# Attention over a cached K and V: keys loaded two units at a time, in even and odd partitions

## The chip, the cores and the metric

The kernel runs on one core of a Trainium2 chip. The metric is the device time of one execution in microseconds (us). Three runs of the kernel before gave 185.0, 185.05 and 185.06 us; the median is 185.05 us. Inside the core, TensorE (PE in the profile) multiplies matrices, VectorE (DVE), ScalarE (ACT) and GpSimd (POOL) work on vectors, and SyncE (SP) issues the transfers, which 16 DMA engines carry out. Each engine works through its own instructions in their order.

## The reference

It is one step of grouped-query attention against a cache: 8 batches with 4 query tokens each, 32 query heads, 8 K/V heads, 2048 cached keys, head size 128, all in bf16.

```python
q = (x @ wq).reshape(B, Sq, Hq, Dh).transpose(0, 2, 1, 3)   # B 8, Sq 4, Hq 32, Dh 128
k = repeat(k_cache, 4, axis=1)                              # k_cache, v_cache: 8, 8, 2048, 128
v = repeat(v_cache, 4, axis=1)
p = softmax(einsum("bhqd,bhkd->bhqk", q, k) * 128 ** -0.5)
o = einsum("bhqk,bhkd->bhqd", p, v)
out = o.transpose(0, 2, 1, 3).reshape(B, Sq, 4096) @ wo     # wo: 4096, 512
```

K and V are 33.5 MB each and wq and wo 4.2 MB each, and every byte is read once.

## The kernel before

The work is cut into NU = 16 units. A unit is one batch with G = 4 K/V heads (half of the eight). Its K fills 128 partitions: partition `g * 32 + s` holds 64 successive keys of head g, 16 KiB in a row of memory. V lies the same way. K has a ring of three buffers in one tile (`k_sb`), V a pool of three (`vpool`).

For a unit, `turn_keys` (L141) has DVE transpose 32x32 blocks of 4-byte words, in NT = 2 instructions of 2048 words a partition; the results go to a pool of three `kt` tiles. `scores` (L211) makes 8 matmuls of 512 columns for each, into a PSUM tile `s_ps` of two banks, of which there are two. `maxima` (L232) takes the row maximum on DVE, `exponentials` (L251) has ACT write the exponentials `s_sb` and their sums `l_sb`. `sums` (L283) adds the two halves' sums on POOL. `probs_to_keys` (L262) transposes `s_sb` on DVE and copies 8 pieces into one of two `probs` tiles, four on ACT and four on POOL. `inverses` (L290) is a reciprocal on DVE that waits for `sums`. `values` (L297) is 32 matmuls of 256 columns against V, in four quarters. `divide` (L317) scales the result on ACT, and `finish` (L327) turns it by a matmul and copies it to `oT` on DVE. At the end the outputs are turned twice more (`to_tokens`, `to_wo_rows`) and multiplied by wo (`project`).

The order on every engine is the order in which the program is written. The main loop (L394) takes one unit a turn. Turn n does `sums(n-1)`, the two `turn_keys(n)`, `scores(n)`, `probs_to_keys(n-1)`, `inverses(n-1)`, `maxima(n)`, `exponentials(n)`, and all of `values(n-2)`. So the scores of a unit stand beside the softmax of the unit before it, and its values come two turns later. Loads are all issued by SP in one queue: K of unit 0, wq, x, K of units 1 and 2, V of unit 0, and then by `load_ready` (L122) K and V in turn, as buffers come free. The last wo rows arrive in pieces of 5, 2 and 1 rows of a partition (L393).

Of the kernel before, what the change touches and what calls it, by code (L numbers as in the profile page):

```python
# [8 lines left out]
BF16 = mybir.dt.bfloat16  # L9
# [5 lines left out]
def kernel(  # L15
# [20 lines left out]
    C = Sk // S  # L36
    HQ = rep * Sq
    NQ = G * HQ
    NT, CT = 2, C // 2
    HP = 8  # L40
    WR = 8
    NP = Hq // HP
    DH = D // 2
    NU = (Hkv // G) * B
    KB, VB, PB, LAG = 3, 3, 2, 2
    XR = 8
    scale = float(Dh) ** -0.5
    AX = mybir.AxisListType.X
# [5 lines left out]
    align.tile([128, 192], BF16, name="pad")  # L54
    wpool = ctx.enter_context(tc.tile_pool(name="wpool", bufs=1))
    kpool = ctx.enter_context(tc.tile_pool(name="kpool", bufs=1))
    vpool = ctx.enter_context(tc.tile_pool(name="vpool", bufs=VB))
    ktpool = ctx.enter_context(tc.tile_pool(name="ktpool", bufs=3))
    const = ctx.enter_context(tc.tile_pool(name="const", bufs=1))
    small = ctx.enter_context(tc.tile_pool(name="small", bufs=2))  # L60
# [5 lines left out]
    order = ctx.enter_context(tc.manual_schedule())  # L66

    wq_sb = wpool.tile([128, R, HqDh], BF16, tag="w", name="wq_sb")
    x_sb = ktpool.tile([128, CT, 2, S, 2], BF16, tag="kt", name="x_sb")
    xT_sb = const.tile([128, R, T], BF16, name="xT_sb")  # L70
    q_bd = const.tile([128, Hkv // G, 2, 2, B, G, HQ], BF16, name="q_bd")
    probs = [const.tile([128, 2, C // 4, 2, G, HQ], BF16, name=f"probs{i}") for i in range(PB)]
# [6 lines left out]
    out_sb = const.tile([T, D], BF16, name="out_sb")  # L79

    units = [(hq, b) for hq in range(Hkv // G) for b in range(B)]
    ks = [None] * NU
    vs = [None] * NU

    k_sb = kpool.tile([128, KB, C, Dh], BF16, name="k_sb")

    def load_k(u, n=1):
        hq, b = units[u]
        nc.sync.dma_start(
            k_sb[:, u % KB : u % KB + n, :, :].rearrange("p b c d -> p b (c d)"),  # L90
            k_cache[b : b + n, G * hq : G * hq + G].rearrange(
                "b g (s c) d -> (g s) b (c d)", c=C
            ),
        )
        for i in range(n):
            ks[u + i] = k_sb[:, (u + i) % KB, :, :]

    def load_v(u):
        hq, b = units[u]
        vs[u] = vpool.tile([128, C, Dh], BF16, tag="v_sb", name="v_sb")  # L100
        of = v_cache[b, G * hq : G * hq + G].rearrange("g (s c) d -> (g s) c d", c=C)
        nc.sync.dma_start(vs[u][:, :, :], of)

    def load_wo(p, r0, n):
        rows = wo[p * HP * 128 : (p + 1) * HP * 128, :].rearrange("(q r) j -> q r j", r=WR)
# [2 lines left out]

    load_k(0)
    nc.sync.dma_start(wq_sb[:, :, :], wq.rearrange("(p r) n -> p r n", r=R))  # L110
    x_all = x_sb[:T, :, :, :, :].rearrange("q c h s e -> q (c h s e)")
    nc.vector.memset(x_all, 0.0)  # L112
    nc.sync.dma_start(x_all[::XR, :], x.flatten_outer_dims().rearrange("(a i) d -> a (i d)", i=XR))
    load_k(1, 2)
    loads = [("v", 0)]
    for u in range(3, NU + 2):
        if u < NU:
            loads.append(("k", u))
        loads.append(("v", u - 2))
    loads.reverse()  # L120

    def load_ready(nk, nv):  # L122
        while loads:
            kind, u = loads[-1]
            if u >= (nk + KB if kind == "k" else nv + VB):
                return
            (load_k if kind == "k" else load_v)(u)
            loads.pop()

    load_ready(0, 0)  # L130

    make_identity(nc, ident[:])
    make_identity(nc, ident4[:])
# [4 lines left out]

    kts = {}

    def turn_keys(u, t):  # L141
        kts[(u, t)] = ktpool.tile([128, CT, 2, S, 2], BF16, tag="kt", name="kt")
        nc.vector.transpose(  # L143
            kts[(u, t)][:, :, :, :, :].rearrange("k c h s e -> k (c h s e)").bitcast(FP32),
            ks[u][:, t * CT : (t + 1) * CT, :].rearrange("s c d -> s (c d)").bitcast(FP32),
        )

    for t in range(NT):
        turn_keys(0, t)

    xtp = psum_m.tile([128, R, T], FP32, tag="m", name="xtp")
    for i in range(XR):
        row = x_all[:, i * D : (i + 1) * D].rearrange("q (p r) -> q r p", r=R)
        for r in range(R):
# [5 lines left out]
                stop=True,  # L160
            )
    nc.vector.tensor_copy(out=xT_sb[:, :, :], in_=xtp[:, :, :])  # L162

    def q_products(hq):
        psq = psum_m.tile([128, rep * Dh], FP32, tag="m", name="psq")
        for r in range(R):
            for g in range(G):
                c0 = (hq * G + g) * rep * Dh
                nc.tensor.matmul(  # L169
                    psq[g * T : (g + 1) * T, :],  # L170
                    lhsT=xT_sb[:, r, :],
                    rhs=wq_sb[:, r, c0 : c0 + rep * Dh],
                    start=(r == 0),
                    stop=(r == R - 1),
                )
        return psq
# [31 lines left out]
    s_pss = {}  # L208
    less = {}

    def scores(u, t):  # L211
        hq, b = units[u]
        if t == 0:
            s_pss[u] = psum_s.tile([128, NT, CT // 2, S], FP32, tag="s", name="s_ps")
        for i in range(4):
            k, e = i // 2, i % 2
            for h in range(2):
                nc.tensor.matmul(  # L218
                    s_pss[u][h * NQ : (h + 1) * NQ, t, :, :],
                    lhsT=q_bd[:, hq, k, e, b, :, :].rearrange("k g q -> k (g q)"),  # L220
                    rhs=kts[(u, t)][:, h * CT // 2 : (h + 1) * CT // 2, k, :, e],
                    start=(i == 0),
                    stop=(i == 3),
                )
# [7 lines left out]
    def maxima(u):  # L232
        top = small.tile([128, 1], FP32, tag="top", name="top")
        swapped = small.tile([128, 1], FP32, tag="swapped", name="swapped")
        less[u] = small.tile([128, 1], FP32, tag="less", name="less")
        nc.vector.reduce_max(  # L236
            out=top[:, :],
            in_=s_pss[u][:, :, :, :].rearrange("q t c s -> q (t c s)"),
            axis=AX,
        )  # L240
        swap_halves(nc.vector, swapped, top)
        nc.vector.tensor_scalar(  # L242
            out=less[u][:, :],
            in0=swapped[:, :],
            scalar1=top[:, 0:1],
            scalar2=-1.0,
            op0=mybir.AluOpType.max,
            op1=MULT,
        )

    def exponentials(u):  # L251
        s_sbs[u] = small.tile([128, C // 4, S, 2], BF16, tag="s_sb", name="s_sb")
        l_sbs[u] = totals.tile([128, 1], FP32, tag="l_sb", name="l_sb")
        nc.scalar.activation(  # L254
            out=s_sbs[u][:, :, :, :].rearrange("q a s j -> q a j s"),
            in_=s_pss[u][:, :, :, :].rearrange("q t (a j) s -> q (t a) j s", j=2),
            func=EXP,
            bias=less[u][:, 0:1],
            accum_out=l_sbs[u][:, :],
        )  # L260
# [22 lines left out]
    def sums(u):  # L283
        swapped = small.tile([128, 1], FP32, tag="l_swapped", name="l_swapped")
        total = small.tile([128, 1], FP32, tag="l_total", name="l_total")
        swap_halves(nc.gpsimd, swapped, l_sbs[u])
        nc.gpsimd.tensor_tensor(out=total[:, :], in0=l_sbs[u][:, :], in1=swapped[:, :], op=ADD)
        return total
# [8 lines left out]
    def values(u, quarter):  # L297
        if quarter == 0:
            o_pss[u] = psum_o.tile([128, 2, Dh], FP32, tag="o", name="o_ps")
        t, h = quarter // 2, quarter % 2  # L300
        for a in range(CT // 4):
            c = quarter * C // 4 + 2 * a
            nc.tensor.matmul(  # L303
                o_pss[u][:, :, :].rearrange("n j d -> n (j d)"),
                lhsT=probs[u % PB][:, h, t * CT // 4 + a, :, :, :].rearrange(
                    "s j g q -> s (j g q)"
                ),
                rhs=vs[u][:, c : c + 2, :].rearrange("s c d -> s (c d)"),
                start=(c == 0),
                stop=(c == C - 2),  # L310
            )
# [78 lines left out]
                    stop=(p == NP - 1 and r == WR - 1),  # L390
                )

    pieces = [(0, 0, 8), (1, 0, 8), (2, 0, 8), (3, 0, 5), (3, 5, 2), (3, 7, 1)]  # L393
    for n in range(NU + LAG):  # L394
        w = n - LAG
        if 0 < n <= NU:
            total = sums(n - 1)
        if 0 < n < NU:
            turn_keys(n, 0)
            turn_keys(n, 1)  # L400
        if n < NU:
            scores(n, 0)
        if w >= 1 and n < NU:
            finish(w - 1)
        if n < NU:
            scores(n, 1)
        if n == 2:
            q_ps = q_products(1)
        if n == 3:
            spread_q(1, q_nat, [by_gpsimd] * G)  # L410
        if 0 < n <= NU:
            probs_to_keys(n - 1)
            inverses(n - 1, total)
        if n < NU:
            maxima(n)
            exponentials(n)
        if n == 2:
            q_nat = scale_q(q_ps)
        if w == B + 1:
            to_tokens(0)  # L420
        if w == B + 2:
            to_wo_rows(0)
        if w >= 0:
            for quarter in range(4):
                values(w, quarter)
            if n >= NU:
                finish(w - 1)
            (divide_all if w == NU - 1 else divide)(w)
        load_ready(min(n + 1, NU), max(w + 1, 0))
        if n == NU - 1:  # L430
            assert not loads, loads
            for piece in pieces:
                load_wo(*piece)

    out_ps = [psum_s.tile([128, DH], FP32, tag="s", name="out_ps") for _ in range(2)]
    half = WR // 2
# [42 lines left out]
```

## Time and profile before

| what | value |
|---|---|
| median of three runs | 185.05 us |
| the profiled execution: its time | 185.0 us |
| its span in the profile | 183.1 us |
| granted TensorE clock, mean | 0.925 |
| bytes read | 75.53 MB, 413 GB/s over the span |
| DMA engines' busy share (data queue) | 97.1% |
| PE, DVE, ACT, POOL busy | 123.2, 121.2, 77.9, 59.3 us |

The page gives the busy time of each engine, the span in 40 slices, the DMA queues, the chain of work that ended last, the costliest groups of instructions (mean time of one, and what ended the idle time before them) and the transfers. The time line gives single instructions with their starts. "Issue to landing" of a transfer includes the time in which it stands behind others.

### The profile page before, as it was taken

The page shows a single profiled execution, that of the slowest core. Times are in us where ns is not written, and L with a number is a line of the kernel's source. Part 1 is how long each engine was busy: PE and PEld are TensorE (multiplying, and loading weights), DVE is VectorE, ACT ScalarE, POOL GpSimd, SP SyncE. Part 2 cuts the span into 40 slices and gives each one's busy share as a digit, 9 for nine tenths or more (in the row PEclk, how much of TensorE's full clock was granted, in tenths as well). Part 3 has the DMA queues.
Part 4 walks back from the last instruction along what each step waited for, and adds up shares of the span by engine and source line. Part 5 has one row for each costly group of instructions (what it writes and reads, how often), then busy time and mean ns, then how long its engine had stood idle before and what let it go on. Part 6 is the DMA issues. An engine that isn't in the chain of part 4 may idle for free.

```text
span 183.1 us, 2559 instructions
## 1 busy us (share of the span) xinstructions
PE 123.2 (67%) x962; PEld 80.4 (44%) x962; DVE 121.2 (66%) x157; ACT 77.9 (43%) x136; POOL 59.3 (32%) x127
## 2 busy tenths in 40 slices
PE   0000652709997978869396878397776978399993
PEld 0000320303664736647154455256463656268872
DVE  6380027797989899894967768576948594946120
ACT  2000112264547748548154544529281719075030
POOL 8900020343237525415151514224240506056000
PEclk9999999995899999999969699969997599969999
DMA  6989999999999999999999999999999999999991
GB/s 182 497 386 419 426 433 429 433 433 426 429 429 437 429 431 420 438 419 437 426 433 429 433 426 437 422 437 433 426 433 429 429 433 426 433 426 422 426 392 49
DMA packets 5666, 75.70 MB, mean 413 GB/s; under 512 B 628, under 2 KB 788, under 8 KB 1044
## 3 DMA queue, kind: packets, MB, share of 16 engines
q1 hardware_dynamic: 5656, 75.57, 97.1%
q8 instruction: 7, 0.11, 0.2%
q14 instruction: 3, 0.02, 0.0%
HBM read 75.53 MB, written 0.03 MB: 413 GB/s over the span
## 4 chain that ended last, share of the span: by engine, by line
DMA 58%; DVE 23%; PE 13%; issue 1%; SPq 1%; POOL 1%; ACT 0%
DMA k_sb<-in_k_cache_dram 38%; DVE kt L143 17%; DMA wo_sb<-in_wo_dram 12%; DMA x_sb<-in_x_dram 8%; PE s_ps L218 6%; PE o_ps L303 4%; DVE top L236 3%; PE psq L169 2%; DVE x_sb L112 1%; SPq L107 1%; POOL q_bd L195 1%; DVE q_t L189 1%; PE out_ps L385 1%; DVE swapped L228 1%; PE xtp L155 1%
## 5 line engine op out<-in xcount | busy, mean ns | idle before, releaser
L143 DVE STREAM_TRANSPOSE kt<-k_sb 128x2048 f32<-128x2048 f32 x32 | 72.0, 2288 | 17.8 <-DMA k_sb<-in_k_cache_dram 17.8
L218 PE MATMUL s_ps<-kt,q_bd 128*64 128x512 bf16 x256 | 44.3, 477 | 37.5 <-DVE kt L143 34.6
L303 PE MATMUL o_ps<-v_sb,probs 128*128 128x256 bf16 x512 | 62.4, 284 | 0.3 <-ACT oT L341 0.3
L274 ACT COPY probs<-p_t 32x512 bf16<-32x512 bf16 x62 | 38.1, 615 | 52.8 <-DVE r_sb L292 51.7
L303 PEld LDWEIGHTS <-probs 128*128 128x128 bf16 x512 | 50.9, 102 | 15.1 <-issue 6.7
L274 POOL COPY probs<-p_t 32x512 bf16<-32x512 bf16 x63 | 38.6, 613 | 56.6 <-DVE r_sb L292 54.3
L218 PEld LDWEIGHTS <-q_bd 128*64 128x64 bf16 x256 | 16.9, 125 | 55.1 <-issue 24.7
L236 DVE TENSOR_REDUCE top<-s_ps 128x1 f32<-128x1024 f32 x16 | 19.6, 1223 | 16.0 <-PE s_ps L218 16.0
L254 ACT ACTIVATE s_sb<-s_ps,less 128x1024 bf16<-128x1024 f32 x16 | 22.4, 1399 | 10.6 <-DVE less L242 10.4
L228 POOL COPY l_swapped<-l_sb 64x1 f32<-64x1 f32 x32 | 5.8, 181 | 32.0 <-ACT s_sb L254 31.3
L155 PE MATMUL xtp<-ident,x_sb 32*128 32x4 bf16 x32 | 1.2, 169 | 18.7 <-DMA x_sb<-in_x_dram 18.7
L323 ACT ACTIVATE o_sc<-o_ps,r_sb 64x128 f32<-64x128 f32 x28 | 10.1, 362 | 7.5 <-PE o_ps L303 6.8
L264 DVE STREAM_TRANSPOSE p_t<-s_sb 128x512 f32<-128x512 f32 x16 | 11.0, 689 | 1.6 <-ACT s_sb L254 1.6
L195 POOL COPY q_bd<-q_t 32x512 bf16<-32x512 bf16 x6 | 3.8, 626 | 18.7 <-DVE q_t L189 18.6
L180 ACT ACTIVATE q_nat<-psq 128x512 bf16<-128x512 f32 x2 | 1.2, 590 | 20.2 <-PE psq L169 20.2
L155 PEld LDWEIGHTS <-x_sb 32*128 32x128 bf16 x32 | 1.1, 112 | 18.7 <-issue 18.7
L340 PEld LDWEIGHTS o_t<-both,o_sc 128*128 128x128 f32 x30 | 4.9, 205 | 6.1 <-issue 4.8
L136 POOL MEMSET probs<- 128x4096 bf16 x2 | 7.0, 3513 | 0.0
L340 PE MATMUL o_t<-both,o_sc 128*128 128x64 f32 x30 | 6.8, 312 | 0.0
L341 DVE CAST oT<-o_t 128x64 bf16<-128x64 f32 x14 | 2.7, 193 | 4.7 <-PE o_t L340 4.7
L228 DVE COPY swapped<-top 64x1 f32<-64x1 f32 x32 | 4.7, 148 | 0.8
L162 DVE CAST xT_sb<-xtp 128x128 bf16<-128x128 f32 x1 | 0.3, 291 | 7.0 <-PE xtp L155 7.0
(37 smaller groups left out, 46.0 us busy)
## 6 DMA issues: line engine op xcount, KB each, us to landing
v_sb<-in_v_cache_dram SPq DMA_DIRECT2D x16, 2048.0 KB, 23.3
k_sb<-in_k_cache_dram SPq DMA_DIRECT2D x14, 2048.0 KB, 23.5
wq_sb<-in_wq_dram SPq DMA_DIRECT2D x1, 4096.0 KB, 17.2
k_sb<-in_k_cache_dram SPq DMA_DIRECT2D x1, 4096.0 KB, 24.3
wo_sb<-in_wo_dram SPq DMA_DIRECT2D x3, 1024.0 KB, 18.9
wo_sb<-in_wo_dram SPq DMA_DIRECT2D x1, 640.0 KB, 21.9
wo_sb<-in_wo_dram SPq DMA_DIRECT2D x1, 256.0 KB, 22.0
wo_sb<-in_wo_dram SPq DMA_DIRECT2D x1, 128.0 KB, 19.6
```

Source lines behind the costliest of these rows:

```text
L136: nc.gpsimd.memset(pr[:, :, :, :, :, :], 0.0)
L143: nc.vector.transpose(kts[(u, t)][:, :, :, :, :].rearrange("k c h s e -> k (c h s e)").bitcast(FP32), ks[u][:, t * CT : (t + 1) * CT, :].r ...
L195: engines[g](out=q_bd[rows, hq, :, :, :, g, :].rearrange("w k e b (h s) -> w (k e b) h s", h=rep), in_=q_t[rows, :, :, :, :].rearrange("w ...
L218: nc.tensor.matmul(s_pss[u][h * NQ : (h + 1) * NQ, t, :, :], lhsT=q_bd[:, hq, k, e, b, :, :].rearrange("k g q -> k (g q)"), rhs=kts[(u, t) ...
L228: engine.tensor_copy(out=out[h * NQ : (h + 1) * NQ, :], in_=in_[(1 - h) * NQ : (2 - h) * NQ, :])
L236: nc.vector.reduce_max(out=top[:, :], in_=s_pss[u][:, :, :, :].rearrange("q t c s -> q (t c s)"), axis=AX,)
L254: nc.scalar.activation(out=s_sbs[u][:, :, :, :].rearrange("q a s j -> q a j s"), in_=s_pss[u][:, :, :, :].rearrange("q t (a j) s -> q (t a ...
L264: nc.vector.transpose(p_t[:, :, :, :, :].rearrange("s x g q j -> s (x g q j)").bitcast(FP32), s_sbs[u][:, :, :, :].rearrange("q a s j -> q ...
L274: by[h * G + g](out=probs[u % PB][g * S : (g + 1) * S, h, :, :, g, :], in_=p_t[quad * S : (quad + 1) * S, :, g % 2, :, :].rearrange("s x q ...
L303: nc.tensor.matmul(o_pss[u][:, :, :].rearrange("n j d -> n (j d)"), lhsT=probs[u % PB][:, h, t * CT // 4 + a, :, :, :].rearrange("s j g q ...
L323: nc.scalar.mul(out=to, in_=of, mul=by)
L340: nc.tensor.matmul(o_t[:, :], lhsT=o_scs[u][:, :], rhs=both[:, :], start=True, stop=True)
```

## The change: K by pairs

A pair is two units, batches b and b + 1 of the same heads. `load_k(p)` now issues two transfers of 64 rows of 32 KiB: unit 2p goes to the even partitions of a buffer and unit 2p + 1 to the odd ones, so each partition holds 128 keys in a row. There are two K buffers of a pair and two V buffers of a unit, each a tile of its own; the bytes of all buffers together are as before. V of units 13 and 14 goes to the K buffer that is free at the end.

`turn_keys(p, t)` is still an instruction over 2048 words a partition, four of them a pair. Its words come out in another order: of every 32 words, the 16 of the even unit are written first and the 16 of the odd unit behind them, so that successive words go to addresses 64 bytes apart in turn. `scores(p, t)` makes 4 matmuls for each of the two units from one `kt` tile. Both `s_ps` tiles are now taken by one pair, and `exponentials` reads its two banks in turn, element by element. The keys' new order is matched in `values`.

The loop takes a pair a turn, with the values of the pair before. `values` of the even unit (`one`) go by quarters between the scores, those of the odd unit (`two`) between the softmaxes. V of units 2p and 2p + 1 is asked for behind turn p's values, and K of pair p + 2 behind those. The last three turns have an order of their own. The last wo rows come as 6 + 2.

```diff
-    NT, CT = 2, C // 2
+    NT, CT = 4, C // 2
+    CP = 2 * C
+    SH = S // 2
-    KB, VB, PB, LAG = 3, 3, 2, 2
+    KB, VB, PB, LAG = 2, 2, 2, 2
+    NPAIR = NU // 2
...
+    k_sb = [kpool.tile([128, CP, Dh], BF16, name=f"k_sb{i}") for i in range(KB)]
+    v_sb = [vpool.tile([128, C, Dh], BF16, name=f"v_sb{i}") for i in range(VB)]
+    spare = k_sb[NPAIR % KB]
+    vs = [v_sb[u % VB][:, :, :] for u in range(NU)]
+    for i, u in enumerate((NU - 3, NU - 2)):
+        vs[u] = spare[:, i * C : (i + 1) * C, :]
+
+    def load_k(p):
+        hq, b = units[2 * p]
+        for i in range(2):
+            nc.sync.dma_start(
+                k_sb[p % KB][i::2, :, :],
+                k_cache[b + i, G * hq : G * hq + G].rearrange("g (s c) d -> (g s) c d", c=CP),
+            )
...
     load_k(0)
     nc.sync.dma_start(wq_sb[:, :, :], wq.rearrange("(p r) n -> p r n", r=R))
-    x_all = x_sb[:T, :, :, :, :].rearrange("q c h s e -> q (c h s e)")
+    x_all = v_sb[0][:T, :, :].rearrange("q c d -> q (c d)")[:, : XR * D]
...
-    load_k(1, 2)
+    load_k(1)
...
+    def turn_keys(p, t):
+        kts[(p, t)] = ktpool.tile([128, CT, 2, 2, SH, 2], BF16, tag="kt", name="kt")
+        words = kts[(p, t)][:, :, :, :, :, :].rearrange("k c w b s e -> k (c w b s e)").bitcast(FP32)
         nc.vector.transpose(
-            kts[(u, t)][:, :, :, :, :].rearrange("k c h s e -> k (c h s e)").bitcast(FP32),
-            ks[u][:, t * CT : (t + 1) * CT, :].rearrange("s c d -> s (c d)").bitcast(FP32),
+            words.rearrange("k (n b s) -> k n s b", b=2, s=SH),
+            k_sb[p % KB][:, t * CT : (t + 1) * CT, :]
+            .rearrange("s c d -> s (c d)")
+            .bitcast(FP32)
+            .rearrange("s (n j b) -> s n j b", j=SH, b=2),
         )
...
-    for t in range(NT):
+    for t in range(3):
         turn_keys(0, t)
...
+    load_v(0)
+    load_v(1)
...
-                    rhs=kts[(u, t)][:, h * CT // 2 : (h + 1) * CT // 2, k, :, e],
+                    rhs=kts[(p, t)][:, :, k, j, :, e],
...
-            in_=s_pss[u][:, :, :, :].rearrange("q t (a j) s -> q (t a) j s", j=2),
+            in_=s_pss[u][:, :, :, :].rearrange("q i c s -> q c s i"),
...
-    pieces = [(0, 0, 8), (1, 0, 8), (2, 0, 8), (3, 0, 5), (3, 5, 2), (3, 7, 1)]
+    pieces = [(0, 0, 8), (1, 0, 8), (2, 0, 8), (3, 0, 6), (3, 6, 2)]
+    def spread(u):
+        total = sums(u)
+        probs_to_keys(u)
+        inverses(u, total)
+    def softmax_top(u):
+        maxima(u)
+        exponentials(u)
...
+    done = None
+    for p in range(NPAIR):
+        last = p == NPAIR - 1
+        one, two = (2 * p - 2, 2 * p - 1) if p else (None, None)
+        if p == NPAIR - 2:
+            two = None
+        if last:
+            one, two = 2 * p - 3, 2 * p - 2
+        for t in range(2):
+            if p:
+                turn_keys(p, t)
+            scores(p, t)
+            if t == 0 and done is not None:
+                finish(done)
...
+        quarters(one, 0, 1)
+        if p:
+            turn_keys(p, 2)
+        scores(p, 2)
+        quarters(one, 2)
+        turn_keys(p, 3)
+        if p == 0:
+            load_k(KB)
+        scores(p, 3)
+        quarters(one, 3)
+        if one is not None:
+            divide(one)
+        softmax_top(2 * p)
+        if last:
+            spread(NU - 3)
+        softmax_top(2 * p + 1)
+        if one is not None:
+            finish(one)
+        if last:
+            quarters(two, 0, 1, 2, 3)
+            divide(two)
+            spread(2 * p)
+        else:
+            spread(2 * p)
+            quarters(two, 0, 1, 2, 3)
+            if two is not None:
+                divide(two)
+            if p != NPAIR - 2:
+                spread(2 * p + 1)
+        done = two
+        if p and p < NPAIR - 2:
+            load_v(2 * p)
+            if p < NPAIR - 3:
+                load_v(2 * p + 1)
+            load_k(p + 2)
+        elif p == NPAIR - 2:
+            load_v(NU - 5)
+            for u in (NU - 4, NU - 3, NU - 2):
+                load_v(u)
+        elif last:
+            load_v(NU - 1)
             for piece in pieces:
                 load_wo(*piece)
+    for w in range(NU - 3, NU):
+        quarters(w, 0, 1, 2, 3)
+        finish(w - 1)
+        (divide_all if w == NU - 1 else divide)(w)
+        if w == NU - 3:
+            spread(NU - 1)
```

## The prediction, made before the changed kernel had run

> **What bounds the kernel now.** I read the page first: the slices, the DMA queues, then the costliest groups.
>
> ```profile
> DMA  6989999999999999999999999999999999999991
> GB/s 182 497 386 419 426 433 429 433 433 426 429 429 437 429 431 420 438 419 437 426 433 429 433 426 437 422 437 433 426 433 429 429 433 426 433 426 422 426 392 49
> q1 hardware_dynamic: 5656, 75.57, 97.1%
> L143 DVE STREAM_TRANSPOSE kt<-k_sb 128x2048 f32<-128x2048 f32 x32 | 72.0, 2288 | 17.8 <-DMA k_sb<-in_k_cache_dram 17.8
> L236 DVE TENSOR_REDUCE top<-s_ps 128x1 f32<-128x1024 f32 x16 | 19.6, 1223 | 16.0 <-PE s_ps L218 16.0
> v_sb<-in_v_cache_dram SPq DMA_DIRECT2D x16, 2048.0 KB, 23.3
> ```
>
> The reader should see that the DMA engines never stop between the first packet and the last, at some 429 GB/s, and that a load stands 23 us behind others: the queue is deep. 75.53 MB at 429 GB/s are 176 us; with 4 us until the stream is under way and 3.1 us from the last wo landing (180.0 us) to the end, that is the span. So the transfers bound it, and compute has a reserve. How large, the time line shows where compute was still catching up. First DVE, then POOL:
>
> ```profile
> 60.98 1.23 DVE L236 TENSOR_REDUCE top<-s_ps 128x1 f32<-128x1024 f32 x1 [0.44 <-PE s_ps L218]
> 62.24 0.31 DVE L228 COPY swapped<-top 64x1 f32<-64x1 f32 x2
> 62.58 0.21 DVE L242 TENSOR_SCALAR less<-swapped,top 128x1 f32<-128x1 f32 x1
> 62.71 4.50 DVE L143 STREAM_TRANSPOSE kt<-k_sb 128x2048 f32<-128x2048 f32 x2
> 67.13 0.19 DVE L341 CAST oT<-o_t 128x64 bf16<-128x64 f32 x1
> 67.24 0.69 DVE L264 STREAM_TRANSPOSE p_t<-s_sb 128x512 f32<-128x512 f32 x1
> 67.85 0.12 DVE L292 RECIPROCAL r_sb<-l_total 128x1 f32<-128x1 f32 x1
> 68.38 1.22 DVE L236 TENSOR_REDUCE top<-s_ps 128x1 f32<-128x1024 f32 x1 [0.40 <-PE s_ps L218]
> ...
> 64.67 0.40 POOL L228 COPY l_swapped<-l_sb 64x1 f32<-64x1 f32 x2 [1.45 <-ACT s_sb L254]
> 65.15 0.19 POOL L287 TENSOR_TENSOR l_total<-l_sb,l_swapped 128x1 f32<-128x1 f32 x1
> 68.09 2.57 POOL L274 COPY probs<-p_t 32x512 bf16<-32x512 bf16 x4 [2.75 <-DVE r_sb L292]
> ```
>
> From maximum to maximum 7.4 us a unit, on DVE almost without a gap: 14.8 us a pair of units, against 19.5 us of transfer. That cover of 4.7 us a pair is what any new wait has to fit into.
>
> **The change, part by part.**
>
> *Rows of 32 KiB.* The trace's packets of 16 KiB take 611 ns (median), wq's of 32 KiB 1213 ns. K goes from 2048 packets to 1024: 2048 x 611 - 1024 x 1213 = 9.2 us of packet time, over 16 engines -0.57 us. The wo end as 6 + 2 saves 128 packets, about 8 ns each by the short rows (1 KiB 46 ns, 2 KiB 84 ns): -0.06 us; four matmuls instead of two follow the last landing, some +0.15 us. Separate tiles move no bytes, and SP issues 40 transfers as it did. All this is worth -0.6 us if the stream stays full.
>
> *The head.* Unit 1's K now stands before x: 2 MiB, 4.8 us. x landed at 18.58 us, and now lands at 23.4. From x to the first scores it was 6.5 us (25.09), so they start at 29.9. Four score blocks follow (8 matmuls took 1.92 us at the low TensorE rate, 1.1 at the high; I take two of each, with the fourth turning fitted in), so the first pair's scores end near 36.5 us. Behind them comes the softmax chain below, 7.9 us here without the o copy: the next pair's first turning starts at 44.4. With its q products (1.9 us) and the first values between, that pair's scores end 13.2 us later, at 57.6. Only 0.9 us later are V0's values done and V2 can be issued, at 58.5. By then the queue is empty: behind x (23.4) come K1 9.7, V0 4.9, V1 4.9, K2 9.7 us, landed by 52.6. A load into an empty queue needs 7.7 us (K of unit 0: issued 0.73, landed 8.42), so V2 lands at 66.2 instead of 57.5. **8.7 us of the stream are lost.** SP stands at V2's wait all that time, with V3 and K3 behind it; nobody asks for K sooner.
>
> *The turn of the loop.* I lay a pair's chain from the start T of its first turning, with rows of the catching-up phase. Scores start 2.36 us after a turning starts (62.71 to 65.07), so at T+2.36. `finish(done)` is behind them on PE (1.02 us on, 0.43 long), and on DVE its o copy stands between the first and second turning: the second starts at T+4.1 where two in a row were 2.2 apart, and its scores at T+6.5. Half the even unit's values are next on PE (16 x 115 ns = 1.84), then the third block (1.1), a quarter (0.92), the fourth block: ended at T+12.45. The turnings on DVE keep ahead of that. Call this end E. Now two maxima (1.8 us each): E+3.6, where before one was on the path. The exponentials: first 2.1 us after E (83.38 to 85.50), 1.3 long; POOL's sum by E+4.4; the o copy and `p_t`: E+4.5; POOL copies four pieces (2.57): E+7.2; only then comes the second unit's sum on POOL (0.4 + 0.2, with gaps): E+7.9, and DVE's reciprocal waits for it, with the next pair's first turning queued behind: T' = E+8.1. Both `s_ps` are the pair's, so no scores can cover that. **A turn is 12.45 + 8.1 = 20.55 us**, above the 19.5 of the stream.
>
> PE stands idle from the odd unit's values (E+6.1) to E+10.5, 4.4 us. After idle times of 2.3 to 2.9 us (89.81, 119.04, 138.51 and 157.89 us) one block took 1.92 us and the values mostly longer (up to 5.43), on average some 1.5 us together; here both lie on the path. **I take 22.0 us a turn** (ends: 20.55, and 23.1 if two blocks and half the values slow down).
>
> *Reads in new patterns.* `exponentials` reads alternate banks. ACT's strided read of `q_nat` (512 elements) took 590 ns, the contiguous `nat` copy 580: I take nothing; at most twice, +1.3 us a turn through the sum. PE reads runs of 16 words instead of 32 at the same step: nothing by L218's rows, which read every second element already.
>
> *Writes in a new pattern.* The turning's successive words go 64 bytes apart. No DVE row does that. Lower end: L143's 2.2 us, with nothing to excuse a gain. Upper: ACT's exponential, which writes every second element, took 1399 ns for 1024 where contiguous rows (256 in 365 ns, 512 in 580) give 1010: a factor 1.4, 3.2 us a turning. I take L143's row, the same operation and size; the other end is a rival.
>
> *The end.* Five turns (pairs 2 to 6) start at 57.6. In turn 6 the odd unit's spread is left out, so the last pair's turning starts 4.6 us after E; no o copy parts its turnings, so its scores end 10.4 us later, with half a microsecond of slow clock 15.5 us after those of pair 6. Behind the last scores stood 21.1 us before (162.0 to 183.1), with two units' values in them; now there are four units' values, two more at 3.67 us: 28.4. The loads of V12 to wo (29.4 us from E+2.5 on) with 4.3 us behind them would end 36 us after E, compute ends after 44.
>
> Sum: 57.6 + 5 x 22.0 + 15.5 + 28.4 = 211.5 us span. Outside the span the profiled execution had 185.0 - 183.1 = 1.9 us, and it stands 0.05 us under the median: **213 us**. With the ends of a turn, 206 to 219.
>
> **The rivals.**
>
> *Hopping writes make DVE slower.* At 3.2 us a turning, the chain's first half grows by about 1 us for each of three turnings: 24.7 us a turn; head +1.7, end +3.5: 59.3 + 123.5 + 47.4 + 1.9 = 232 us. For it: the exponential's factor. Against: that row may owe it to the function. The Trainium skill, Vector Engine (DVE) Microarchitecture Reference, section Measured stream behaviour on trn2, gives a write that hops with every element 1.71 ns a column instead of 1.05, and 2.5 for a small step; no run here shows it. By 1.71 it would be, as an estimate, 3.6 us a turning and 243 us in all; by 2.5, over 265. The same section has a read that alternates between two regions at the full rate, so the rule leaves it open.
>
> *Half the partitions slow the loads.* Each K transfer fills every second partition. If two engines then meet at one place, a packet takes up to 2.43 instead of 1.21 us; a pair's loads grow from 19.5 to 29 us, and 8 pairs give 185 + 77 = 262 us. Nothing in the trace speaks for it: wq's rows are as long at full rate, but go to all partitions.
>
> *Only the head is lost.* If the turns fit into 19.5 us after all (the clock stays high, waits overlap), the stream loses 8.7 us alone: 184.4 + 8.7 = 193 us.
>
> *Not slower.* The stream stays full and only the packets count: 185.0 - 0.6 = 184.4 us. It decides where V2 is issued before 50 us and a turn stays under 19.5. The reserve of 4.7 us a pair speaks for it; the second maximum, the POOL queue and x's delay against.
>
> **How the numbers follow.** Chances: forecast 0.47, hopping writes 0.31, slow loads 0.08, head alone 0.07, not slower 0.05, others (slower) 0.02. The forecast's own range is 206 to 219. The range over all goes down to the head alone, 193, and up to the hopping writes with a turn at its slow end (5 x 1 us more) and half of the banks' dearest reading on top (8 x 0.8 us): 244. It leaves out the slow loads and the not slower, and a little of the hopping writes. Faster by over 0.2% (what a measurement of this kernel can tell) 0.04, within 0.2% 0.01, slower 0.95.
>
> **What would show it.** In the profile of the changed kernel: x landing near 23.4 us and the DMA slices with a gap near 52 to 60 us, then small gaps in each turn; V's issue waiting for `values` and not for a buffer's load; about 22 us from one pair's first turning to the next; the reciprocal waiting for POOL; the mean of the turning's row near 2290 ns (3200 or more: the first rival); 32 KiB packets at 1.21 us (more: the second). A DMA row of nines throughout would prove me wrong.

## The result, and the profile after

The changed kernel takes 240.65 us (median of six runs, 239.19 to 241.32), against 185.06 us for the kernel before on the same chip: a ratio of 1.2991, with a 95% interval from 1.295 to 1.3032. The profiled execution spans 239.2 us, at a mean granted TensorE clock of 0.800 (0.925 before). Two of the four executions of each of two kernels below were slower ones, and differences go by the other two: 226.40 and 228.62 us with plain writes, 204.72 and 207.23 us with the hop alone.

From the page of the kernel after, its slices, its data queue and the groups that answer to those shown before; below them the scores' group of the kernel before:

```profile
PEclk9999998557995599656995699558975595589999
DMA  7999999950499919994599829992799639929960
q1 hardware_dynamic: 4504, 75.57, 77.1%
L129 DVE STREAM_TRANSPOSE kt<-k_sb 128x2048 f32<-128x2048 f32 x32 | 113.2, 3614 | 11.4 <-DMA k_sb<-in_k_cache_dram 8.3
L212 PE MATMUL s_ps<-kt,q_bd 128*64 128x512 bf16 x256 | 47.4, 506 | 73.5 <-DVE kt L129 70.5
L248 ACT ACTIVATE s_sb<-s_ps,less 128x1024 bf16<-128x1024 f32 x16 | 22.4, 1398 | 12.6 <-DVE less L236 12.3
v_sb<-in_v_cache_dram SPq DMA_DIRECT2D x14, 2048.0 KB, 9.0
```

```profile
L218 PE MATMUL s_ps<-kt,q_bd 128*64 128x512 bf16 x256 | 44.3, 477 | 37.5 <-DVE kt L143 34.6
```

The DMA row has a hole in every turn of the loop where it had nines from end to end. The queue is busy for 77.1% of the span instead of 97.1%, and V lands 9.0 us after its issue (the median) instead of 23.3: little stands in front of it. So compute sets the pace, and the row that has grown is the turning of the keys: 3614 ns each instead of 2288, 113.2 us instead of 72.0. PE waits 70.5 us for turned keys, where it was 34.6.

One boundary between two turns, on DVE and POOL, from the time line of the kernel after (start and duration in us; in brackets the idle time before, and what ended it; shorter rows between these are left out):

```profile
87.64 1.22 DVE L230 TENSOR_REDUCE top<-s_ps 128x1 f32<-128x1024 f32 x1 [1.12 <-PE s_ps L212]
89.37 1.22 DVE L230 TENSOR_REDUCE top<-s_ps 128x1 f32<-128x1024 f32 x1
92.78 0.71 DVE L258 STREAM_TRANSPOSE p_t<-s_sb 128x512 f32<-128x512 f32 x1 [0.76 <-ACT s_sb L248]
95.42 0.16 DVE L286 RECIPROCAL r_sb<-l_total 128x1 f32<-128x1 f32 x1 [1.93 <-POOL l_total L281]
95.50 3.61 DVE L129 STREAM_TRANSPOSE kt<-k_sb 128x2048 f32<-128x2048 f32 x1
...
92.09 2.56 POOL L268 COPY probs<-p_t 32x512 bf16<-32x512 bf16 x4 [0.27 <-DVE r_sb L286]
94.71 0.40 POOL L222 COPY l_swapped<-l_sb 64x1 f32<-64x1 f32 x2
95.19 0.19 POOL L281 TENSOR_TENSOR l_total<-l_sb,l_swapped 128x1 f32<-128x1 f32 x1
```

This is the wait that the prediction laid out: two maxima, then the reciprocal of the odd unit behind POOL's sum, which stands behind POOL's four copies; the next pair's turning is queued behind it. From the end of the scores to that turning it is 95.50 - 87.64 = 7.86 us. The next turnings of this kind start at 122.23, 148.22 and 174.69 us, 26.4 us apart on average.

What SP's queue waited for most, in the kernel after (total us, times, longest):

```profile
SPq L101 <- PE o_ps L297: 155.0, 12, 24.2
```

In the loop the V loads wait until `values` has read their buffers; for earlier V transfers they wait 9.6 us in all. That is how the turn's length becomes a hole in the stream. The first hole is the head's: the prediction had the queue empty at 52.6 us and V2 issued at 58.5, and V2 was issued at 62.09.

### The profile page after: what moved, and what is told of

Its sections match the earlier page's. It is cut to its first block, busy times and chain, and to the rows that moved or that the text cites. A ratio compares the mean times of both kernels' runs of the same rounds, so it can differ in the third digit from the quotient of the medians.

```text
span 239.2 us, 2556 instructions
## 1 busy us (share of the span) xinstructions
PE 132.4 (55%) x962; PEld 82.4 (34%) x962; DVE 163.5 (68%) x157; ACT 77.3 (32%) x136; POOL 59.1 (25%) x127
## 3 DMA queue, kind: packets, MB, share of 16 engines
q1 hardware_dynamic: 4504, 75.57, 77.1%
## 4 chain that ended last, share of the span: by engine, by line
PE 42%; DVE 37%; DMA 9%; POOL 6%; issue 3%; ACT 1%; POOLq 0%; ACTq 0%
DVE kt L129 28%; PE o_ps L297 21%; PE s_ps L212 14%; DMA v_sb<-in_x_dram 9%; DVE top L230 4%; POOL probs L268 4%; PE o_t L334 2%; PE out_ps L379 2%; PE psq L160 2%; ACT o_sc L317 1%; DVE swapped L222 1%; DVE p_t L258 1%; POOL l_swapped L222 1%; DVE v_sb L113 1%; DVE less L236 1%
## 5 line engine op out<-in xcount | busy, mean ns | idle before, releaser
L129 DVE STREAM_TRANSPOSE kt<-k_sb 128x2048 f32<-128x2048 f32 x32 | 113.2, 3614 | 11.4 <-DMA k_sb<-in_k_cache_dram 8.3
L212 PE MATMUL s_ps<-kt,q_bd 128*64 128x512 bf16 x256 | 47.4, 506 | 73.5 <-DVE kt L129 70.5
L297 PEld LDWEIGHTS <-probs 128*128 128x128 bf16 x512 | 52.5, 107 | 19.6 <-issue 10.0
L212 PEld LDWEIGHTS <-q_bd 128*64 128x64 bf16 x256 | 17.4, 133 | 93.3 <-issue 73.8
L230 DVE TENSOR_REDUCE top<-s_ps 128x1 f32<-128x1024 f32 x16 | 19.5, 1219 | 12.7 <-PE s_ps L212 12.7
L248 ACT ACTIVATE s_sb<-s_ps,less 128x1024 bf16<-128x1024 f32 x16 | 22.4, 1398 | 12.6 <-DVE less L236 12.3
L144 PE MATMUL xtp<-ident,v_sb 32*128 32x4 bf16 x32 | 1.2, 169 | 23.7 <-DMA v_sb<-in_x_dram 23.7
L286 DVE RECIPROCAL r_sb<-l_total 128x1 f32<-128x1 f32 x16 | 2.5, 157 | 12.5 <-POOL l_total L281 12.5
L334 PE MATMUL o_t<-both,o_sc 128*128 128x64 f32 x30 | 7.5, 339 | 6.2 <-ACT o_sc L317 6.2
L334 PEld LDWEIGHTS o_t<-both,o_sc 128*128 128x128 f32 x30 | 5.5, 230 | 12.2 <-ACT o_sc L317 8.1
L144 PEld LDWEIGHTS <-v_sb 32*128 32x128 bf16 x32 | 1.1, 112 | 23.7 <-issue 23.7
L297 PE MATMUL o_ps<-k_sb,probs 128*128 128x256 bf16 x64 | 7.3, 273 | 0.1
```

The lines of the kernel that those rows point to most:

```text
L129: nc.vector.transpose(words.rearrange("k (n b s) -> k n s b", b=2, s=SH), k_sb[p % KB][:, t * CT : (t + 1) * CT, :] .rearrange("s c d -> s ...
L212: nc.tensor.matmul(s_pss[u][h * NQ : (h + 1) * NQ, t // 2, :, :], lhsT=q_bd[:, hq, k, e, b, :, :].rearrange("k g q -> k (g q)"), rhs=kts[( ...
L230: nc.vector.reduce_max(out=top[:, :], in_=s_pss[u][:, :, :, :].rearrange("q i c s -> q (i c s)"), axis=AX,)
L248: nc.scalar.activation(out=s_sbs[u][:, :, :, :].rearrange("q a w j -> q a j w"), in_=s_pss[u][:, :, :, :].rearrange("q i c s -> q c s i"), ...
L297: nc.tensor.matmul(o_pss[u][:, :, :].rearrange("n j d -> n (j d)"), lhsT=probs[u % PB][:, h, a0 + a, :, :, :].rearrange("s j g q -> s (j g q)"
L334: nc.tensor.matmul(o_t[:, :], lhsT=o_scs[u][:, :], rhs=both[:, :], start=True, stop=True)
```

## The experiments

The theory after the result: the loss has two parts. The words that go to addresses 64 bytes apart in turn (the hop, below) make the turning 1.6 times as long; and the order of the waits (head, two softmaxes in a row, four units' values at the end) holds a turn above the stream even with the old turning. The rival is that the hop matters little, and all of it is the order, or the reads of the two banks, or the loads into every second partition.

### Plain writes in the kernel after

```diff
-        kts[(p, t)] = ktpool.tile([128, CT, 2, 2, SH, 2], ...)
+        kts[(p, t)] = ktpool.tile([128, CT, 2, SH, 2, 2], ...)
         nc.vector.transpose(
-            words.rearrange("k (n b s) -> k n s b", b=2, s=SH), ...
+            kts[(p, t)]...rearrange("k c w s b e -> k (c w s b e)").bitcast(FP32), ...
...
-                    rhs=kts[(p, t)][:, :, k, j, :, e],
+                    rhs=kts[(p, t)][:, :, k, :, j, e],
```

> The changed kernel with one part undone: the turnings write their 32 words of a block one behind the other, and PE picks a unit's words with a step of two words instead. Theory (the hopping write makes a turning 3.6 us instead of 2.2, and the rest of the loss is the pair's chain of waits): the turning's row goes back to some 2290 ns, a turn of the loop takes about 23 us instead of 26.5, and the time is about 217 us (210 to 221), still far above 185. Rival A (the hopping write is the whole loss): about 185 us. Rival B (it is the order of the waits alone, the longer turning only fills idle time): above 235 us. If PE pays for reading every second word, its score blocks get longer than 1.9 and 1.0 us.

Measured: 229.21 us (226.4 to 230.26), 1.2403 of the kernel before [1.2372, 1.2433]. Its turnings and scores, from the groups of this kernel:

```profile
L128 DVE STREAM_TRANSPOSE kt<-k_sb 128x2048 f32<-128x2048 f32 x32 | 71.9, 2286 | 11.8 <-DMA k_sb<-in_k_cache_dram 8.6 <-PE s_ps L208 3.2
L208 PE MATMUL s_ps<-kt,q_bd 128*64 128x512 bf16 x256 | 61.8, 619 | 53.2 <-ACT probs L264 28.4 <-DVE kt L128 21.7 <-POOL q_bd L182 2.9
```

The turning is back at 2286 ns, as expected, but the time is some 10 us above the 217 expected, and above the range of 210 to 221. PE's new way of reading has a price: it takes every second word (a step of 8 bytes), and its time line shows score blocks of 1.90 us directly beside quarters of the values that take 1.05, all at a granted clock of 1.00 (130.2 to 133.1 us):

```profile
127.36 1.98 PE L208 MATMUL s_ps<-kt,q_bd 128*64 128x512 bf16 x8
129.27 1.05 PE L293 MATMUL o_ps<-v_sb,probs 128*128 128x256 bf16 x8
130.25 1.90 PE L208 MATMUL s_ps<-kt,q_bd 128*64 128x512 bf16 x8
132.08 1.05 PE L293 MATMUL o_ps<-v_sb,probs 128*128 128x256 bf16 x8
```

In the kernel after, which reads at a step of 4 bytes, twelve of the score blocks in these places (the third and fourth of a turn, turns 1 to 7) take 1.05 or 1.06, and the other two 1.18 and 1.39. So this run moves one cost from DVE to PE, and does not yet separate the hop from the order. Three more did.

### The hop alone, and runs of two words, in the kernel before

The kernel before with the changed kernel's order of writes:

```diff
+        words = kts[(u, t)]...rearrange("k c h s e -> k (c h s e)").bitcast(FP32)
         nc.vector.transpose(
-            kts[(u, t)]...rearrange("k c h s e -> k (c h s e)").bitcast(FP32),
-            ks[u][...]...rearrange("s c d -> s (c d)").bitcast(FP32),
+            words.rearrange("k (n b s) -> k n s b", b=2, s=S // 2),
+            ks[u][...]....bitcast(FP32).rearrange("s (n j b) -> s n j b", j=S // 2, b=2),
```

> The kernel before with nothing but the writing order of the turnings changed: of every 32 words the even ones first, the odd ones behind them, so successive words go 64 bytes apart. The scores read the tile as before, so keys stand in another order than V's and the output is not the reference's; no work is left out. Theory: the turning takes 3.6 us, a unit's chain on DVE grows from 7.4 to 10.05 us and passes the 9.75 us of a unit's loads: 28.8 + 3 x 10.9 + 12 x 10.05 + 21.1 + 1.9 = about 205 us (200 to 208). Rival (the long turning in the changed kernel comes from the loads into every second partition or from anything else of the pair's form): the row stays at 2290 ns and the time at 185 us.

Measured: 207.64 us (204.72 to 208.28), 1.1128 [1.1075, 1.1182]; the group of this kernel:

```profile
L144 DVE STREAM_TRANSPOSE kt<-k_sb 128x2048 f32<-128x2048 f32 x32 | 114.0, 3636 | 3.1 <-DMA k_sb<-in_k_cache_dram 3.1
```

3636 ns, and the kernel goes from its bound by transfers to a bound by DVE, which holds 66% of the chain that ended last, where it was 23%. The hop alone costs some 21 us here (206.0 against 185.1), with nothing else changed; the long turning needs neither pairs nor loads into every second partition. Then the same with two neighbouring words between hops:

```diff
-            words.rearrange("k (n b s) -> k n s b", b=2, s=S // 2),
+            words.rearrange("k (n b q r) -> k n q b r", b=2, q=8, r=2),
```

> As the kernel with hopping writes before, but with two neighbouring words between hops: words 0 and 1, then 16 and 17, then 2 and 3, and so on. The output is again not the reference's, and no work is left out. Theory (a write costs more only where a word stands alone; the Trainium skill, Vector Engine (DVE) Microarchitecture Reference, section Measured stream behaviour on trn2, has runs of two adjacent words at the full rate): the turning's row at 2290 ns and 185 us. Rival (every hop of 64 bytes costs, so half as many hops cost half): about 2.95 us a turning, 8.7 us a unit on DVE, still under the loads' 9.75: 185 to 188 us with the row at 2950 ns; so the row decides, not the time.

Measured: 185.06 us (184.96 to 185.35), 0.9999 [0.999, 1.0007]; the group:

```profile
L144 DVE STREAM_TRANSPOSE kt<-k_sb 128x2048 f32<-128x2048 f32 x32 | 72.0, 2289 | 18.1 <-DMA k_sb<-in_k_cache_dram 18.1
```

At this distance of 64 bytes the jump itself is free; what costs is that every single word stands alone. Runs of two 4-byte words cost what contiguous writes cost.

### The kernel after with runs of two words

A unit's words lie in runs of two if its K goes to two neighbouring partitions out of four. That keeps the rows of 32 KiB, the order of the work and PE's step:

```diff
-        for i in range(2):
-            nc.sync.dma_start(k_sb[p % KB][i::2, :, :], k_cache[b + i, ...] ...)
+        for i in range(4):
+            rows = k_cache[b + i // 2, G * hq : G * hq + G].rearrange("g (s c) d -> (g s) c d", c=CP)
+            nc.sync.dma_start(k_sb[p % KB][i::4, :, :], rows[i % 2 :: 2, :, :])
...
-            words.rearrange("k (n b s) -> k n s b", b=2, s=SH),
+            words.rearrange("k (n b m r) -> k n m b r", b=2, m=SH // 2, r=2),
```

> The changed kernel in its own order, with K put in by two partitions as in the run before, and nothing else. Theory: the sum on record with its turning at 2.2 us: first pair's scores end near 35.6 us, the second's near 57, a turn near 22 to 23 us, and about 213 us (209 to 217); what is missing to the changed kernel's 240.7 is the price of the hopping write. Rival (the waits fit under the loads once the turning is short): below 195 us.

Measured: 218.51 us (217.29 to 219.77), 1.1804 [1.1754, 1.1854]; span 215.2. Slices and turnings of this kernel, and the DVE rows around two starts of a turn:

```profile
DMA  7999999994299969998699959996799939999960
L127 DVE STREAM_TRANSPOSE kt<-k_sb 128x2048 f32<-128x2048 f32 x32 | 71.9, 2288 | 11.6 <-DMA k_sb<-in_k_cache_dram 8.3 <-PE s_ps L210 3.2
```

```profile
87.20 2.31 DVE L127 STREAM_TRANSPOSE kt<-k_sb 128x2048 f32<-128x2048 f32 x1
92.24 0.23 DVE L333 CAST oT<-o_t 128x64 bf16<-128x64 f32 x1 [2.72 <-PE o_t L332]
92.38 6.69 DVE L127 STREAM_TRANSPOSE kt<-k_sb 128x2048 f32<-128x2048 f32 x3
102.55 1.22 DVE L228 TENSOR_REDUCE top<-s_ps 128x1 f32<-128x1024 f32 x1 [3.48 <-PE s_ps L210]
...
110.33 0.16 DVE L284 RECIPROCAL r_sb<-l_total 128x1 f32<-128x1 f32 x1 [1.93 <-POOL l_total L279]
110.51 2.31 DVE L127 STREAM_TRANSPOSE kt<-k_sb 128x2048 f32<-128x2048 f32 x1
```

The turn shown takes 110.51 - 87.20 = 23.3 us, 15.35 to the maxima and 7.96 from there. The time is 1.5 us above the range expected, the turning as expected. The hop's share in the kernel after is 240.65 - 218.51 = 22.1 us; the other 33.4 us are there without it, and the holes in the DMA row are still one a turn.

### Another order of the waits

Here the order is changed as well, so that the waits named in the prediction leave the path: wq and x are loaded before K, the reciprocal of the odd unit goes behind the next pair's first turning, the o copy behind the fourth turning, and V and K are asked for as soon as each buffer is read. The diff shows the core of it. Three kernels differ only in how the words go: plain writes with PE's step of 8 bytes, the hop, and runs of two words (with K in two neighbouring partitions out of four, as above).

```diff
-    load_k(0)
     nc.sync.dma_start(wq_sb...)
     nc.sync.dma_start(x_all[::XR, :], ...)
+    load_k(0)
     load_k(1)
...
             if p:
                 turn_keys(p, t)
+            if t == 0 and pending is not None:
+                inverses(*pending)
             scores(p, t)
-            if t == 0 and done is not None:
-                finish(done)
...
+        if done is not None:
+            finish(done)
         scores(p, 3)
...
+        if 1 < p < NPAIR - 2:
+            load_v(2 * p)
+            load_k(p + 2)
...
-                spread(2 * p + 1)
+                pending = spread(2 * p + 1, later=True)
```

Plain writes:

> The pair kernel with plain writes and the waits of the loop moved: wq and x are loaded ahead of the first K; the reciprocal of a pair's odd unit stands behind the next pair's first turning; the o copy stands behind the fourth turning; V and K of the next pairs are asked for in the order V, K, V, the first as soon as its buffer's values are done; in the second pair all the values come before the third block. 32 KiB rows, buffers and the wo end of 6 + 2 stay. Theory (without hopping writes and these waits a turn needs about 16.5 us and hides under the 19.5 us of its loads, and the head loses nothing): DMA slices of nines to the end and 184.4 to 187 us. Rival (pairs need more buffers than there are: the queue runs empty whatever the order): above 190 us, with gaps in the DMA slices in each turn.

Measured: 199.31 us (198.16 to 200.26), 1.0771 [1.0743, 1.0799].

The hop:

> The new order of the kernel before, but with the hopping writes of the changed kernel (and so PE reading runs of 16 words at the usual step). Theory (a turn is the four turnings, 3 x 3.51 + 3.75, the last block 1.1, and 5.8 us of softmax on DVE up to the next turning): 21.1 us a turn; first pair's scores end at 38 us, the seventh's at 165, the last's at 185, with 25.6 us behind them: 212 us (206 to 216); so the moved waits give back some 28 of the 55 us and the writes keep the rest. Rival (the order is worth nothing where DVE is the slowest): above 230 us.

Measured: 215.52 us (213.7 to 216.12), 1.1653 [1.1627, 1.1679].

Runs of two words:

> The new order, with a pair's K put into the buffer by two partitions: partitions 0 and 1 of every four hold two rows of the even unit, 2 and 3 two rows of the odd one (four transfers of 32 rows of 32 KiB a pair). So the turning writes two neighbouring words between hops, and PE reads runs of 16 words at the usual step. Theory (both prices are gone: the turning at 2290 ns as in the run with pairs of words, blocks at 1.1 and 1.9 us): a turn needs about 16.5 us, less than its 19.5 us of loads; DMA slices of nines, 184.4 to 186.5 us. Rival A (32-row transfers of every fourth partition load slower): packets of 32 KiB above 1.22 us, and above 190 us. Rival B (two buffers of a pair are too few, the queue runs empty in every turn): 187 to 196 us with dips in the DMA slices.

Measured: 191.74 us (191.19 to 192.04), 1.0354 [1.0337, 1.0371]. Slices of this last kernel, and PE's waits for V in its time line:

```profile
DMA  6999998999999997999999899999999999999930
```

```profile
94.81 5.15 PE L294 MATMUL o_ps<-v_sb,probs 128*128 128x256 bf16 x32 [4.12 <-DMA v_sb<-in_v_cache_dram]
114.27 5.65 PE L294 MATMUL o_ps<-v_sb,probs 128*128 128x256 bf16 x32 [5.18 <-DMA v_sb<-in_v_cache_dram]
133.56 6.23 PE L294 MATMUL o_ps<-v_sb,probs 128*128 128x256 bf16 x32 [3.69 <-DMA v_sb<-in_v_cache_dram]
```

The plain and the two-word kernel both missed what was expected of them, up to 187 and 186.5 us; the 191.74 lies where the rival of two buffers too few had put it (187 to 196). The kernel with the hop came in its range. The order recovers 218.51 - 191.74 = 26.8 of the 33.4 us. The hop costs 215.52 - 191.74 = 23.8 us in this order, and PE's step 199.31 - 191.74 = 7.6 us. What is left over the kernel before is 6.7 us. The trace shows two places for it: V of the odd unit can be asked for only when its buffer has been read (at 76.78 us, behind the four transfers of K from 71.78 on), and PE waits for it until 94.81 with the next pair's scores behind, 13.4 us in four such waits; and 25.7 us of the span stand behind the last scores, where it was 21.1. How the 6.7 us divide between them was not tested. A third V buffer, with the rows kept, was not run, so whether K by pairs can beat the kernel before stays open.

### The wo end, and PE's step by itself

In the kernel before, the last wo rows as 6 + 2:

```diff
-    pieces = [(0, 0, 8), (1, 0, 8), (2, 0, 8), (3, 0, 5), (3, 5, 2), (3, 7, 1)]
+    pieces = [(0, 0, 8), (1, 0, 8), (2, 0, 8), (3, 0, 6), (3, 6, 2)]
```

> The kernel before with nothing but the last wo rows as 6 + 2 instead of 5 + 2 + 1. Theory: 128 packets less are worth -0.06 us, two more matmuls behind the last landing +0.15 us: 185.1 us, within 0.2 us of the kernel before. Rival (the last piece's own completion counts): 0.5 us or more to either side.

Measured: 185.29 us (185.16 to 185.35), 1.001 [1.0001, 1.0018]. That is no gain. The +0.2 us would fit the four matmuls behind the last landing (+0.15 us in the prediction) against the packets (-0.06), but nothing here shows it to be them.

PE's step by itself, in the kernel before:

```diff
-                    rhs=kts[(u, t)][:, h * CT // 2 : (h + 1) * CT // 2, k, :, e],
+                    rhs=kts[(u, t)][:, :, k, h::2, e],
```

> The kernel before, its turnings untouched; a scores matmul takes every second word of all the turned words (a step of 8 bytes) where it took all words of half of them (a step of 4 bytes). The keys then stand in another order than V's, so the output is not the reference's; the amount of work is the same. Theory (TensorE takes its moving operand at half the rate when the step is 8 bytes): a block of 8 matmuls takes 1.9 to 2.0 us at the high clock too, where the kernel before has blocks of about 1.05. On the chain of a unit stands one block behind the second turning, so 7.4 us become 8.3, still under the stream's 9.75: 185.0 to 186.5 us in all. Rival (the long blocks of the kernel after with plain writes came from the low granted clock): blocks stay near 1.05 us wherever the values' quarters take about 1, and the time is 185.05.

Measured: 185.09 us (184.99 to 185.41), 0.9999 [0.999, 1.0009]. PE's time line of this kernel, and a block of the kernel before that stands beside values of 3.67 us too:

```profile
131.00 1.94 PE L218 MATMUL s_ps<-kt,q_bd 128*64 128x512 bf16 x8
133.48 3.67 PE L303 MATMUL o_ps<-v_sb,probs 128*128 128x256 bf16 x32
140.77 1.90 PE L218 MATMUL s_ps<-kt,q_bd 128*64 128x512 bf16 x8
142.60 3.67 PE L303 MATMUL o_ps<-v_sb,probs 128*128 128x256 bf16 x32
```

```profile
150.39 1.13 PE L218 MATMUL s_ps<-kt,q_bd 128*64 128x512 bf16 x8 [0.73 <-DVE kt L143]
```

Every block now takes 1.9 to 2.1 us, while the values beside them stay at 3.67, as at the high clock before; the granted clock is 1.00 from 120 to 150 us, and 0.981 on average, above the 0.925 of the kernel before. So the way of reading is the cause and not the clock. What in it costs is not separated: in this run, as with plain writes, the two matmuls that take turns through a block also read alternate words of the same stretch, each at its step of 8 bytes. The time of the kernel doesn't change: its reserve of 4.7 us a pair is larger than the 1.6 us a pair (0.8 a unit) that stand on the chain.

## Why the prediction was right in sign and 28 us low

**The step that failed is "Writes in a new pattern".** It took 2.2 us a turning from the row of the same operation, and put the hop's price into a rival with an upper end of 3.2 us, from ACT's exponential. Measured: 3.61 to 3.64 us, in three kernels, and 2.28 to 2.29 with runs of two. ACT's row was the wrong measure for DVE. The rest of the mechanism held: with runs of two words, the prediction's own kernel without the price of the hop, the span is 215.2 us, 3.7 above the 211.5 of the sum.

The range over all, up to 244, held the result by luck. It was the rival's 232 us at 3.2 us a turning, 5 us for slow turns, and 6.4 us for reading the banks in turn, which cost nothing. These 6.4 us stood in for the 0.4 us a turning by which ACT's row was short; without them the range would have ended at 237.

The rival's estimate by the Trainium skill (Vector Engine (DVE) Microarchitecture Reference, section Measured stream behaviour on trn2: 1.71 ns a column for a write that hops 4 KiB with every element) was 3.6 us a turning and 243 us in all. The trace agrees, with 3614 ns and 240.65 us, for a hop of 64 bytes; the rival's own terms, put up from 1.0 to 1.4 us a turning, give 240. The 2.5 ns that the prediction gave from that section for a small step were not reached: 3614 ns are 1.76 ns a column. The statement in the same section that runs of two or more words hop for nothing agrees with the trace too, with 2289 ns.

By the prediction's own steps, in us of the span:

| step | predicted | after | runs of two words |
|---|---|---|---|
| x landed | 23.4 | 23.60 | 24.07 |
| end of the first pair's scores | 36.5 | 36.89 | 35.98 |
| next pair's first turning | 44.4 | 44.59 | 43.79 |
| end of that pair's scores | 57.6 | 61.11 | 56.47 |
| V2 issued | 58.5 | 62.09 | 57.44 |
| a turn | 22.0 | 26.5 | 23.6 |
| of it, scores to the next turning | 8.1 | 7.86 | 7.96 |
| pair 6's scores to pair 7's | 15.5 | 20.0 | 15.3 |
| behind the last scores | 28.4 | 25.6 | 25.7 |

(Of "a turn", 26.5 is the time between the ends of the scores of pairs 1 and 6, 193.60 - 61.11, over five, and 23.6 is 174.26 - 56.47 over five.) The differences from the prediction add up: in the kernel after 3.5 + 22.5 + 4.5 - 2.8 = 27.7 us, which is 239.2 - 211.5; with runs of two words -1.1 + 7.8 - 0.2 - 2.7 = 3.8, against 215.2 - 211.5 = 3.7.

- *The head* is right to 0.4 us up to the second pair's turnings. There the hop tells: four turnings in a row take 14.08 us (8.89 with runs of two words), and the scores end 3.5 us after the forecast, where with runs of two they end 1.1 before it.
- *The turn of the loop*: the wait chain from the scores to the next turning was forecast at 8.1 and measured at 7.86, with the reciprocal behind POOL (1.93 us) as laid out. The other half was forecast at 12.45 and, with the slow clock's share, 13.9; it took 15.6 on average even with the short turnings. The trace of that run shows 1.92 us for both score blocks that follow a wait, and the o copy held until 5.04 us into the turn, so that the second turning starts at 5.18 where 4.1 had been worked out. With 23.6 us a turn, the forecast's upper end of 23.1 was a little short even without the hop.
- *Reads in new patterns*: nothing was taken, and nothing shows. The exponential, which reads the two banks in turn, takes 1398 ns against 1399 before, and PE's blocks on runs of 16 words go at 1.05 us.
- *Rows of 32 KiB*: each packet takes 1213 ns (median of 1152, 95% up to 1221), as wq's did. The rival of slow loads is ruled out: into every second and every fourth partition the packets take 1213 ns. The -0.57 us can't be seen in a stream with holes, and no run tried the rows by themselves; the wo end alone gained nothing.
- *The end* was forecast 2.8 us too dear: it took 25.6 us. The sum took the 21.1 us of the kernel before for two units' values and added two more; its time line has three units' values behind the last scores (96 matmuls from 161.93 us on). With one more of 3.67 us the sum would have been 24.8. The four units' values of the kernel after stand one behind another at 3.66 us each.
- *Only the head is lost* and *not slower* needed turns under 19.5 us, and the runs have 23.6 even without the hop. The new order with runs of two words comes nearest, and even that ends at 191.74 us.

## What to carry to other kernels

When a tuned kernel rests on a small reserve (here 4.7 us a pair of units), lay the changed chain out operation by operation, and price each new access pattern by a row of the same engine or, where there is none, give its dearer price the greater weight: a write order cost 22 us, and 27 us more came back when the waits were ordered anew, while all that the longer rows could save was estimated under 1 us. A layout that scatters single words may be kept by scattering neighbouring pairs of words, as it was here. And before moving an awkward step from one engine to another, price it there too: the same words, read by PE at twice the step, took its blocks from 1.05 to 1.90 us.

## What the runs showed of the hardware

- DVE's 128x2048 turning of 4-byte words takes 3614 to 3636 ns when successive words go 64 bytes apart, and 2277 to 2289 ns with plain writes or with runs of two words 64 bytes apart.
- PE, reading its moving operand (bf16, 512 columns), takes 1.9 us for a block of eight matmuls at a step of 8 bytes, with the block's two halves on alternate words, against 1.05 to 1.1 at a step of 4 bytes, both at a granted clock of 1.00. At a granted clock of 0.50 the step of 4 bytes has blocks of 1.92 too (kernel after, 99.2 to 101.1 us).
- ACT reads two PSUM banks in turn, element by element, at no cost: 1398 against 1399 ns for 1024 elements a partition.
- Packets of 32 KiB to every second or fourth partition take 1213 ns (median), as to all partitions.
